# A token and channel mixer on one core: the steady part in 64-row tiles, two streams on different PSUM banks

## Chip, core and metric

The kernel runs on one core of one Trainium2 chip. The metric is the device time of one execution in microseconds; lower is better. Three runs of the kernel before gave 2051.5, 2051.76 and 2052.26 us, so the median is 2051.76 us.

## What is computed

Input `x` is 8 batches of 4096 tokens of 192 channels. First a causal local mix over 7 taps with softmaxed weights per head, then a token mix and a channel mix with ReLU, each added to what it was given. Cut to what matters:

```python
w = exp(weight_gen - max); w = w / (sum(w) + 1e-9)      # 8 heads, 7 taps
a = einsum('bshk,bskhg->bshg', w, x_unf)                # x_unf: 7 rows back from each token
h = maximum(a.transpose(0, 2, 1) @ w_tok1, 0) @ w_tok2  # 4096 -> 256 -> 4096
u = a + h.transpose(0, 2, 1)
out = u + maximum(u @ w_ch1, 0) @ w_ch2                 # 192 -> 1536 -> 192
```

The four weight matrices are float64; the kernel reads them as pairs of 32-bit words and makes float32 of them on the chip ("convert").

## The kernel before, in words

The work is cut into 64 chunks `g` of 512 tokens (8 to a batch). Every number that enters a matmul is split into a high and a low float32r part, and a product is the sum of high by high, low by high and high by low. One step on TensorE is 512 columns of one such product.

A chunk has these TensorE stages. **First channel product** (`channel1`, L735): the 1536 hidden units are 6 groups `p` of two 128-blocks; the 192 channels are three 64-row blocks. For each `p` there are 9 pairs of 64-row matmuls, one half of the array for each 128-block, each half writing its own bank of the tile `ph` (two banks). Since both halves need all 192 channels, `u` is held with its blocks copied to both halves (`u_parts`, L692: eight casts on ScalarE, two subtractions on VectorE). **Token product 2** (`token2`, L628): 10 matmuls of 128 rows into `up`, for the next chunk; ScalarE writes a seed into the tile first. **Sums** (`channel2`, L768): 10 matmuls of 128 rows for each `p`, into two accumulator banks `acc`. **Token product 1** (`token1`, L588): 16 matmuls of 128 rows and 384 or 192 columns into `th`, for a chunk of the next batch; there is one such piece a chunk until the last batch. For batch 1 (`b < F1`) it is done in plain float32 (`token1_float`, L620); the columns of a bank that a piece doesn't use are written once by extra matmuls (L608).

Between first product and sums stands `take_h` (L761): ScalarE writes the ReLU as the high part, VectorE the low part, into one of `HB` = 4 tiles `h`. `ph`, `up` and `th` share a ring of three two-bank PSUM tiles; with the two `acc` banks all eight are taken. At the end of a chunk VectorE transposes `acc` (`store`, L829) and ScalarE seeds it with the next `u` (`seed`, L822).

Order: the loop from L1324 writes each chunk's order by hand: all six first products, then token product 2 where it is ready, then the sums, with a token-1 piece where its data are ready (`picks`, L1308). In chunk 0 the first two groups are done together (`first_channel1`, L747). All engines run in program order. A planner that runs in Python while the program is built (`at`, `on`, `pump`, L868 to L978) keeps an estimate of each engine's time and fits the rest (softmax and taps for the next batch, conversions, stores) into the gaps of ScalarE and VectorE; VectorE may be filled up to `SLACK` (1500 ns) past a ReLU.

Chunk 0 runs while weights are still being converted. What is left to convert is hung on the groups `p` in a table: after `take_h` of group `p`, `run_first(p)` (L1244) puts these steps on ScalarE ("a"), VectorE ("v") and GpSimd:

```python
c21, w21, c22 = ("c2", 1), ("w2", 1), ("c2", 2)
first = {0: ((w1[2], ""),), 1: ((c2, "aa"), (c2, "v")), 2: ((c2, ""), (c21, "a")),
         3: ((c21, "aa"), (c21, "v"), (w21, "aaa"), (c21, ""), (w21, "v")),
         4: ((w21, ""), (c22, "aa")), 5: ((c22, "a"), (c22, "vw")), NP: ((c22, ""),)}
```

`w1` is the first channel matrix in three thirds, `c2` to `c22` the thirds of the second (groups 0 and 1, 2 and 3, 4 and 5), `w21` the token-2 weights of chunk 1; "" means all that is left.

Of the kernel before, what the change touches and what calls it, by code (L numbers as in the profile page):

```python
# [18 lines left out]
AX = mybir.AxisListType  # L19


@with_exitstack
def mixer_kernel(ctx: ExitStack, tc: tile.TileContext, x, wg, wt1, wt2, wc1, wc2, out):
# [14 lines left out]
    HB = 4  # L38
# [28 lines left out]
    TURN = (0, 1, 2), (1, 0, 2)  # L67
# [472 lines left out]
    def fetch_channel(which, n, tag=None):  # L540
        raw = raw_tile(tag)
        queue = nc.sync
        if which == "w1":
            dst = raw[:, 0:HF, :].rearrange("p (k n) l -> p k (n l)", k=3)
            src = wc1.rearrange("(k c) (j q n) -> j c k q n", k=3, q=NP // NC1, j=2)
            for j in range(2):
                queue.dma_start(dst[j * DC:(j + 1) * DC], src[j, :, :, n])
        else:
            c2_dma(queue, raw[:, 0:NF2 * D, :], n)
        rawt[which, n] = raw  # L550
        tag_of[which, n] = raw_tag.get(staged["raw"] - 1)
# [35 lines left out]

    def token1(m):  # L588
# [8 lines left out]
        yield  # L597
        if b >= F1:
            xh = xht.pop(m)
            for r in range(KR):  # L600
                for c in range(CT):
                    rs = slice(r * P, (r + 1) * P)
                    nc.tensor.matmul(th[:, r, 0:2 * D], w[:, c, 0, rs], xh[:, c, :], start=i + c == 0, stop=False,  # L603
                                     skip_group_check=True)
                    nc.tensor.matmul(th[:, r, 0:D], w[:, c, 1, rs], xh[:, c, 0:D], start=False, stop=c == CT - 1,  # L605
                                     skip_group_check=True)
                if m == F1 * NCH:
                    nc.tensor.matmul(th[:, r, 2 * D:], w[:, CT - 1, 0, rs], xh[:, 0, 0:N - 2 * D],  # L608
                                     start=False, stop=True, skip_group_check=True)
        else:  # L610
            token1_float(th, w, m, 0 if i == 0 else None, CT - 1)
        yield
# [6 lines left out]

    def token1_float(th, w, m, first, last):  # L620
        for r in range(KR):
            for c in range(CT):
                nc.tensor.matmul(th[:, r, 0:D], w[:, c, r * P:(r + 1) * P], xat[m][:, c, :],  # L623
                                 start=c == first, stop=c == last, skip_group_check=True)
# [3 lines left out]
    def token2(m):  # L628
# [4 lines left out]
        yield  # L633
        steps = [(n, k, d, l) for n, of in ((0, ((A_HI, 0), (A_HI, 1), (A_LO, 0))), (1, ((C_HL, 0), (C_HL, 1))))
                 for k in range(KR) for d, l in of]
        if m == 1:
            steps.sort(key=lambda s: s[3])
        for i, (n, k, d, l) in enumerate(steps):
            nc.tensor.matmul(up[:, n, :], h1[:, k, d], w[:, l, k * N:(k + 1) * N], start=False,  # L639
                             stop=n not in [s[0] for s in steps[i + 1:]], skip_group_check=True)  # L640
        yield
# [29 lines left out]

    def first_u(up):

        hi, lo = (late.tile([P, 3, N], F32R, tag=x, name=x) for x in ("u_hi", "u_lo"))
        c, e = slice(0, DC), slice(DC, P)
        uc = uf_[0][:, 1, :]
        f, g, act, dve = lo.bitcast(F32), hi.bitcast(F32), nc.scalar.copy, nc.vector
        act(hi[:, 0], up[0])
        dve.tensor_sub(lo[:, 0], up[0], hi[:, 0].bitcast(F32))
        act(hi[c, 1], g[e, 0])  # L680
        act(hi[e, 1], g[c, 0])
        dve.tensor_copy(uc[c], up[1][e])
        act(lo[c, 1], f[e, 0])
        dve.tensor_add(uc[c], up[1][c], uc[c])
        dve.tensor_copy(lo[e, 1], f[c, 0])
        act(hi[c, 2], uc[c])
        dve.tensor_copy(hi[e, 2], uc[c])
        dve.tensor_sub(lo[c, 2], uc[c], hi[c, 2].bitcast(F32))
        dve.tensor_copy(lo[e, 2], f[c, 2])
        ut[0] = hi, lo  # L690

    def u_parts(m):  # L692
# [3 lines left out]
        hi, lo = (late.tile([P, 3, N], F32R, tag=x, name=x) for x in ("u_hi", "u_lo"))  # L696
        f, act, dve = lo.bitcast(F32), nc.scalar.copy, nc.vector.tensor_sub
        left = [0, 1]
        taken = {}

        def begin():
            yield "gate", 0, lambda: state["channel1"] >= m
            yield "w", 0, lambda: free["parts"]

        def last():
            left.pop()
            if not left:
                ut[m] = hi, lo
                free["u"] = at["act"] + HOP

        def first():
            yield from begin()
            yield "u", 620, lambda: act(hi[:, 0], ua)
            yield "u", 620, lambda: act(hi[c, 2], uc[c])
            yield "n", 0, lambda: taken.update(at=at["act"] + HOP)
            yield "v", 610, lambda: dve(lo[:, 0], ua, hi[:, 0].bitcast(F32))
            yield "v", 610, lambda: dve(lo[c, 2], uc[c], hi[c, 2].bitcast(F32))
            yield "u", 620, lambda: act(lo[c, 1], f[e, 0])
            yield "u", 620, lambda: act(lo[e, 1], f[c, 0])
            yield "u", 620, lambda: act(lo[e, 2], f[c, 2])  # L720
            yield "n", 0, last

        def second():
            yield from begin()
            yield "gate", 0, lambda: "at" in taken
            yield "u", 620, lambda: act(hi[c, 1], ua[e])
            yield "u", 620, lambda: act(hi[e, 1], ua[c])
            yield "u", 620, lambda: act(hi[e, 2], uc[c])
            yield "n", 0, last
        return first(), second()  # L730


    ht, acc_t = {}, {}

    def channel1(g, p):  # L735

        u_hi, u_lo = ut[g]
        ph = ps_w.tile([P, 2, 512], F32, tag="w", name="ph")
        steps = [(w, u, k) for w, u in ((w1_hi, u_hi), (w1_lo, u_hi), (w1_hi, u_lo)) for k in range(3)]
        for n, (w, u, k) in enumerate(steps):  # L740
            for j in range(2):
                rows = slice(j * DC, (j + 1) * DC)
                nc.tensor.matmul(ph[:, j, :], w[rows, TURN[j][k], p * P:(p + 1) * P], u[rows, k], start=n == 0,  # L743
                                 stop=n == len(steps) - 1)
        return ph

    def first_channel1(ps):  # L747

        u_hi, u_lo = ut[0]
        ph = {p: ps_w.tile([P, 2, 512], F32, tag="w", name="ph") for p in ps}  # L750
        for k in range(3):
            for steps in (((w1_hi, u_hi), (w1_lo, u_hi)), ((w1_hi, u_lo),)):
                for p in ps:
                    for w, u in steps:
                        for j in range(2):
                            rows = slice(j * DC, (j + 1) * DC)
                            nc.tensor.matmul(ph[p][:, j, :], w[rows, TURN[j][k], p * P:(p + 1) * P], u[rows, k],
                                             start=k == 0 and w is w1_hi and u is u_hi, stop=k == 2 and u is u_lo)
        return ph

    def take_h(g, p, ph):  # L761
        h = ht[g, p] = big.tile([P, 2, 2, N], F32R, tag=f"h{(g * NP + p + 2) % HB}", name="h")
        nc.scalar.activation(h[:, :, 0, :], ph, AF.Relu)  # L763
# [683 lines left out]
```

## Time and profile before

| what | value |
|---|---|
| median of three runs | 2051.76 us |
| span of the profiled execution | 2049.8 us |
| TensorE matmuls busy | 2036.6 us, 99% |
| VectorE, ScalarE busy | 73%, 70% |
| GpSimd busy | 10% |
| mean granted TensorE clock | 1.000 |

The profile is of one execution. A line of a view names engine (PE is TensorE's matmuls, PEld its weight loads, DVE VectorE, ACT ScalarE, POOL GpSimd, SP the DMA queue of SyncE), source line, operation, what is written and read, and how often. Starts are microseconds from the start of the span. Ends of matmuls are modelled, so times between starts are the safe ones. A wait is given in brackets with what ended it; "issue" means that the profile shows nothing that the engine waited for.

### The profile page before, as it was taken

How to read it: one execution, taken by the hardware profiler on the slowest of the kernel's cores; microseconds unless marked ns; L12 is line 12 of the kernel's file. 1: busy time of each engine (PE TensorE's matmuls, PEld its weight loads, DVE VectorE, ACT ScalarE, POOL GpSimd, SP SyncE). 2: the span in 40 equal slices, each digit the busy share in tenths (PEclk: the TensorE clock that was granted, in tenths of full speed). 3: DMA queues.
4: the chain of work that ended last, by engine and by line, in shares of the span. 5: the costliest groups of instructions: out<-in, count | busy, mean ns of one | idle time of the engine just before them, and what ended most of it. 6: DMA issues, size and time to landing. Idle time of an engine off the chain costs nothing.

```text
span 2049.8 us, 32333 instructions
## 1 busy us (share of the span) xinstructions
PE 2036.6 (99%) x12893; PEld 1682.0 (82%) x12893; DVE 1502.7 (73%) x1740; ACT 1439.2 (70%) x2286; POOL 195.6 (10%) x260
## 2 busy tenths in 40 slices
PE   8999999999999999999999999999999999999999
PEld 8888888888888888888888888888888888888887
DVE  9979989999877787776877777877777774434343
ACT  6888767677667677677676676676676676676665
POOL 1201111111110110100110101110001110000000
PEclk9999999999999999999999999999999999999999
DMA  9948787887876666666666666766666753222121
GB/s 342 353 159 220 194 231 226 214 247 220 226 211 182 182 186 177 186 177 180 185 180 176 187 171 176 200 175 169 172 188 179 198 145 98 90 72 65 45 65 24
DMA packets 172662, 362.32 MB, mean 177 GB/s; under 512 B 28639, under 2 KB 113887, under 8 KB 156766
## 3 DMA queue, kind: packets, MB, share of 16 engines
q1 hardware_dynamic: 137342, 225.91, 35.6%
q0 software_dynamic: 34880, 134.10, 26.7%
q8 instruction: 101, 1.65, 0.3%
q14 instruction: 51, 0.42, 0.1%
q10 hardware_dynamic: 288, 0.23, 0.0%
HBM read 223.60 MB, written 71.30 MB: 144 GB/s over the span
## 4 chain that ended last, share of the span: by engine, by line
PE 94%; DVE 4%; DMA 1%; ACT 0%; issue 0%; POOL 0%; ACTq 0%; DVEq 0%
PE acc L775 41%; PE ph L743 38%; PE up L639 7%; PE th L603 4%; PE th L605 2%; DVE prk L408 1%; PE th L623 1%; PE tapsum L414 1%; DMA space<-in_x_dram 1%; PE th L1111 0%; PE acc L792 0%; DVE h L764 0%; DVE pr L266 0%; DVE vals L191 0%; DMA wg<-in_weight_gen_dram 0%
## 5 line engine op out<-in xcount | busy, mean ns | idle before, releaser
L775 PE MATMUL acc<-h,w2s 128*128 128x512 f32 x3800 | 884.7, 390 | 0.1
L775 PEld LDWEIGHTS acc<-h,w2s 128*128 128x128 f32 x3800 | 709.2, 188 | 146.5 <-issue 0.7
L763 ACT ACTIVATE h<-ph 128x1024 fp32r<-128x1024 f32 x384 | 394.3, 1027 | 345.9 <-PE ph L743 306.0
L764 DVE SCALAR_TENSOR_TENSOR h<-ph,h 128x1024 fp32r<-128x1024 f32 x384 | 468.2, 1220 | 175.7 <-ACT h L763 175.2
L743 PE MATMUL ph<-u_hi,w_hi 64*128 64x512 f32 x2292 | 330.7, 393 | 0.9 <-DVE h L764 0.9
L743 PE MATMUL ph<-u_lo,w_hi 64*128 64x512 f32 x2292 | 323.2, 387 | 0.0
L743 PE MATMUL ph<-u_hi,w_lo 64*128 64x512 f32 x2292 | 322.9, 387 | 0.0
L266 DVE TENSOR_TENSOR pr<-space,wg 128x768 f32<-128x768 f32 x336 | 311.0, 947 | 0.6
L288 POOL DMA_DIRECT2D xa<-pr x166 | 141.5, 854 | 1350.6 <-DVE pr L280 608.2
L743 PEld LDWEIGHTS ph<-u_hi,w_hi 64*128 64x128 f32 x2292 | 209.9, 184 | 65.1 <-issue 20.9
L743 PEld LDWEIGHTS ph<-u_hi,w_lo 64*128 64x128 f32 x2292 | 215.0, 184 | 46.3
L743 PEld LDWEIGHTS ph<-u_lo,w_hi 64*128 64x128 f32 x2292 | 215.2, 184 | 45.5
L846 ACT COPY out_tile<-oa 32x256 f32<-32x256 f32 x504 | 203.5, 404 | 8.1
L646 DVE TENSOR_TENSOR uf<-up,uf 64x512 f32<-64x512 f32 x63 | 43.0, 683 | 201.9 <-ACT uf L645 201.9
L639 PE MATMUL up<-w,h 128*128 128x512 f32 x630 | 161.4, 402 | 0.0
L280 DVE TENSOR_TENSOR pr<-pr 128x768 f32<-128x768 f32 x168 | 159.1, 947 | 2.3
L639 PEld LDWEIGHTS up<-w,h 128*128 128x128 f32 x630 | 114.0, 188 | 41.4 <-issue 18.3
L603 PE MATMUL th<-xh,w 128*128 128x384 f32 x384 | 112.4, 358 | 0.0
L846 ACT COPY out_tile<-oc 32x256 f32<-32x256 f32 x252 | 101.7, 403 | 4.9 <-DVE oc L839 0.4
L836 DVE STREAM_TRANSPOSE oa<-acc 128x512 f32<-128x512 f32 x63 | 45.0, 715 | 81.8 <-PE acc L775 81.8
L656 ACT COPY up<-xb 128x1024 f32<-128x1024 f32 x56 | 57.0, 1018 | 63.3 <-DVE h L764 63.3
L605 PE MATMUL th<-xh,w 128*128 128x192 f32 x384 | 96.2, 250 | 0.0
(130 smaller groups left out, 1721.9 us busy)
## 6 DMA issues: line engine op xcount, KB each, us to landing
w<-s SPq DMA_DIRECT2D x96, 1024.0 KB, 5.9
xa<-pr POOLq DMA_DIRECT2D x166, 384.0 KB, 4.8
space<-in_x_dram POOLq DMA_DIRECT2D x54, 960.0 KB, 7.9
out_dram<-out_tile SPq DMA_DIRECT2D x128, 192.0 KB, 4.0
xb<-xs SPq DMA_DIRECT2D x368, 64.0 KB, 5.0
xs<-t SPq DMA_DIRECT2D x56, 384.0 KB, 4.7
raw<-in_moe_w_tok_dram SPq DMA_DIRECT2D x16, 1024.0 KB, 8.1
s<-w POOLq DMA_DIRECT2D x8, 1024.0 KB, 8.6
```

The lines of the kernel that those rows point to most:

```text
L266: nc.vector.tensor_mul(t.rearrange("p t (h g) -> p (t h) g", h=H).rearrange("p (o n) g -> p o n g", o=1), x_k, w)
L280: nc.vector.tensor_add(sums[m], sums[m], prt.pop(m))
L288: nc.gpsimd.dma_start(xat[m].rearrange("p t d -> p (t d)"), sums[m].rearrange("p t d -> p (t d)"), accum_op=ALU.add)
L603: nc.tensor.matmul(th[:, r, 0:2 * D], w[:, c, 0, rs], xh[:, c, :], start=i + c == 0, stop=False, skip_group_check=True)
L605: nc.tensor.matmul(th[:, r, 0:D], w[:, c, 1, rs], xh[:, c, 0:D], start=False, stop=c == CT - 1, skip_group_check=True)
L639: nc.tensor.matmul(up[:, n, :], h1[:, k, d], w[:, l, k * N:(k + 1) * N], start=False, stop=n not in [s[0] for s in steps[i + 1:]], skip_gr ...
L656: nc.scalar.copy(up.rearrange("p k (n b c) -> p (k n) c b", c=CT, b=Q), xb.rearrange("p k (n c b) -> p (k n) c b", c=CT, b=Q))
L743: nc.tensor.matmul(ph[:, j, :], w[rows, TURN[j][k], p * P:(p + 1) * P], u[rows, k], start=n == 0, stop=n == len(steps) - 1)
L763: nc.scalar.activation(h[:, :, 0, :], ph, AF.Relu)
L764: nc.vector.scalar_tensor_tensor(h[:, :, 1, :], ph, 0.0, h[:, :, 0, :].bitcast(F32), op0=ALU.max, op1=ALU.subtract)
L775: nc.tensor.matmul(acc[n], w2s[:, f, d], h[:, j, l, :], start=False, stop=f == NF - 1 and i == len(steps) - 1, skip_group_check=True)
L846: nc.scalar.copy(dst, src[to:to + Q].rearrange("p (n e d) -> p n e d", n=2, d=Q)[:, n])
```

## The change

The whole steady part is done in 64-row tiles. Two streams run side by side, one on rows 0 to 63 and one on rows 64 to 127, and at any step they write different PSUM banks. A 128-row matmul becomes two 64-row ones, one in each stream, at different times.

- `emit` writes two lists of steps pairwise. Where a bank passes from one half to the other it demands more than `GAP` = 3 steps between, and puts a no-operation on TensorE's queue that waits for the old half's last matmul, unless an earlier one covers it.
- A first product has three parts (`h_steps`): each half's own 64 channels into its own bank, the last 64 channels (held in both halves), and the same own channels for the other bank. So the first two blocks of `u` need no copy in the other half; `u_parts` has four casts on ScalarE in place of eight. The rows of the first channel weights are laid out to fit (`fetch_channel`).
- A unit of the steady part is one first product beside the sums of an older group: 19 steps. One unit has token product 2 in place of the first product (20 steps). The units of a chunk are products 3, (token 2), 4, 5, and 0 and 1 of the next chunk, beside sums 0 to 5. Product 2 comes between chunks, with a token-1 piece around it or, without one, together with product 3 and sums 0 (28 steps).
- A token-1 piece is cut into two halves that stand before and after a unit.
- `HB` is 3; `u` of odd chunks takes the place of the fourth `h` tile.
- In chunk 0, products 0 to 2 come first (27 steps), then units (3, 0), (4, 1), (token 2, 2), (5, 3) and the next chunk's.

The table `first` and `run_first` are as before. The diff, cut to its core:

```diff
-    HB = 4
+    HB = 3
...
             for j in range(2):
-                queue.dma_start(dst[j * DC:(j + 1) * DC], src[j, :, :, n])
+                rows = dst[j * DC:(j + 1) * DC]
+                queue.dma_start(rows[:, 0:2], src[j, :, j:3:2 - j, n])
+                queue.dma_start(rows[:, 2], src[1 - j, :, j, n])
...
+    SIDES = [slice(j * DC, (j + 1) * DC) for j in range(2)]
+    used = {}
+    GAP = 3
+
+    def emit(*sides):
+
+        assert len(sides[0]) == len(sides[1])
+        for steps in zip(*sides):
+            used["n"] = used.get("n", 0) + 1
+            for j, (bank, out_, w, x_, start) in enumerate(steps):
+                side, n, before_ = used.get(bank, (j, 0, None))
+                if side != j:
+                    assert used["n"] - n > GAP
+                    if n > used.get("past", 0):
+                        tc.add_manual_dep(nc.tensor.nop().ins, before_.name, SYNC, reason="bank")
+                        used["past"] = n - 1
+                ins = nc.tensor.matmul(out_, w, x_, start=start, stop=False, skip_group_check=True).ins
+                used[bank] = j, used["n"], ins
...
+        def steps(n, of, j):
+            rows = SIDES[j]
+            return [(("up", m, n), up[:, n, :], h1[rows, k, d], w[rows, l, k * N:(k + 1) * N], False)
+                    for d, l in of for k in range(KR)]
...
+        yield "u", 620, lambda: act(hi[:, 0], ua)
+        yield "u", 620, lambda: act(hi[c, 1], uc[c])
+        yield "u", 620, lambda: act(hi[e, 1], uc[c])
+        yield "v", 610, lambda: dve(lo[:, 0], ua, hi[:, 0].bitcast(F32))
+        yield "v", 610, lambda: dve(lo[c, 1], uc[c], hi[c, 1].bitcast(F32))
+        yield "u", 620, lambda: act(lo[e, 1], lo[c, 1].bitcast(F32))
...
-    def channel1(g, p):
+    def h_steps(g, p, ahead):
...
+        def steps(j, at_, block, bank, start):
+            rows = SIDES[j]
+            return [(("ph", g, p, bank), ph[:, bank, :], w[rows, at_, p * P:(p + 1) * P], u[rows, block], start and i == 0)
+                    for i, (w, u) in enumerate(((w1_hi, u_hi), (w1_lo, u_hi), (w1_hi, u_lo)))]
+        own = [steps(j, 0, 0, j, j == 0 or not ahead) for j in range(2)]
+        third = [steps(j, 1, 1, j, False) for j in range(2)]
+        other = [steps(j, 2, 0, 1 - j, ahead and j == 0) for j in range(2)]
+        return ph, own, third, other
...
-    def channel2(g, p):
+    def sum_steps(g, p):
...
     for g in range(NG):
...
+        units = [(3, 0), (None, 1), (4, 2), (5, 3), (NP, 4), (NP + 1, 5)]
+        if g == 0:
+            units[1:3] = [(4, 1), (None, 2)]
+            hs = [first_product(0, p) for p in range(3)]
+            own, third, other = zip(*[h["parts"] for h in hs])
+            order = [own[0], own[1], other[0], other[1], own[2], third[0], other[2], third[1], third[2]]
+            emit(*[list(chain(*[part[j] for part in order])) for j in range(2)])
...
+            if tok is not None:
+                emit(*[h["own"][j] + tok["steps"](j, SIDES[j], True) + h["other"][j] + tok["steps"](1 - j, SIDES[j], False)
+                       for j in range(2)])
...
+                emit(both[0] + h["other"][0] + sums[0][1] + more["other"][0] + sums[0][0],
+                     both[1] + sums[1][0] + h["other"][1] + more["other"][1] + sums[1][1])
...
+            if hp is None:
+                ends.append(up_next["t"])
+                us = up_next["sides"]
+                sides = [us[0][0] + us[0][1] + sums[0][1] + sums[0][0], sums[1][1] + sums[1][0] + us[1][0] + us[1][1]]
...
+                turned = sums[1][1] + sums[1][0] + h["other"][1] + h["own"][1]
+                sides = [h["own"][0] + h["other"][0] + sums[0][1] + sums[0][0], turned]
+            if tok is not None:
+                ends.append(tok["t"])
+                sides = [tok["steps"](j, SIDES[j], True) + sides[j] + tok["steps"](1 - j, SIDES[j], False) for j in range(2)]
+            emit(*sides)
...
+                take(h, done_at, turn)
+                pump(at["dve"] + 1000, soon, free["acc"] + HOP)
+                seed(g + 1)
```

## Rows read from the trace of the kernel before

**Rows 1.** The page: engines' busy time (share of span), and granted clock in slices.
```profile
PE 2036.6 (99%) x12893; PEld 1682.0 (82%) x12893; DVE 1502.7 (73%) x1740; ACT 1439.2 (70%) x2286; POOL 195.6 (10%) x260
...
PEclk9999999999999999999999999999999999999999
```

**Rows 2.** The chain that ended last, in order of time: start, length, what.
```profile
999.35 6.80 PE acc L775 x30
...
1008.40 6.83 PE acc L775 x30
1015.23 12.49 PE ph L743 x108
1027.72 2.51 PE up L639 x10
...
1846.70 12.49 PE ph L743 x108
...
1875.30 12.49 PE ph L743 x108
```

**Rows 3.** Timeline of one `ph` stage: start, length, engine, what, xcount.
```profile
1015.16 0.97 PE L743 MATMUL ph<-u_hi,w_hi 64*128 64x512 f32 x6
...
1015.97 0.85 PE L743 MATMUL ph<-u_hi,w_lo 64*128 64x512 f32 x6
...
1018.04 0.84 PE L743 MATMUL ph<-u_hi,w_lo 64*128 64x512 f32 x6
...
1018.72 0.84 PE L743 MATMUL ph<-u_lo,w_hi 64*128 64x512 f32 x6
...
1019.60 1.03 ACT L763 ACTIVATE h<-ph 128x1024 fp32r<-128x1024 f32 x1 [0.17 <-PE ph L743]
```

**Rows 4.** Waits of the weight loads: total us, times, longest.
```profile
PEld ph L743 <- issue: 20.9, 60, 0.4
```

**Rows 5.** One line's instructions: duration ns min/median/max, first and last start.
```profile
L639 PEld LDWEIGHTS up<-w,h x630: 186/188/189, 103.3 to 2004.1; 128*128 128x128 f32 x158
...
L639 PEldq EVENT_SEMAPHORE  x57: 51/51/3631, 99.4 to 1999.6; - x57
```

**Rows 6.** Timeline of VectorE in chunk 0: weights, low parts.
```profile
87.10 0.96 DVE L211 TENSOR_TENSOR w_lo<-val,w_hi 128x768 fp32r<-128x768 f32 x1
...
92.84 1.22 DVE L764 SCALAR_TENSOR_TENSOR h<-ph,h 128x1024 fp32r<-128x1024 f32 x1
93.97 0.41 DVE L566 TENSOR_TENSOR w2s<-val,w2s 128x256 fp32r<-128x256 f32 x1
...
105.14 0.95 DVE L191 SCALAR_TENSOR_TENSOR val<-val,few 128x768 uint32<-128x768 uint32 x1
...
107.83 0.41 DVE L566 TENSOR_TENSOR w2s<-val,w2s 128x256 fp32r<-128x256 f32 x1
```

**Rows 7.** Busy time in one stretch: engines in order PE, PEld, DVE, ACT, POOL.
```profile
170.00:204.00 34.00, 34.00 (x212) 28.30 (x210) 32.20 (x40) 28.34 (x42) 5.09 (x7) 1.00 0.94 269
```

**Rows 8.** Timeline at a chunk's end and start: transpose of `acc`, its two seeds.
```profile
1015.27 0.72 DVE L836 STREAM_TRANSPOSE oa<-acc 128x512 f32<-128x512 f32 x1 [0.64 <-PE acc L775]
...
1022.69 1.11 ACT L827 COPY acc<-uf 128x512 f32<-128x512 f32 x2
```

**Rows 9.** Timeline of TensorE: the first product of chunk 0 and of chunk 1.
```profile
83.15 0.50 PE L757 MATMUL ph<-u_hi,w_hi 64*128 64x512 f32 x2
...
113.08 0.97 PE L743 MATMUL ph<-u_hi,w_hi 64*128 64x512 f32 x6
```

**Rows 10.** Timeline of ScalarE in chunk 0: conversions and the seed of `up`.
```profile
93.80 1.10 ACT L194 ACTIVATE few<-raw 128x768 f16<-128x768 f32 x1
...
95.52 1.15 ACT L192 ACTIVATE few<-raw 128x1024 uint32<-128x1024 uint32 x1
...
97.95 1.13 ACT L195 ACTIVATE val<-raw 128x1024 f32<-128x1024 f32 x1
...
101.96 1.05 ACT L654 COPY up<-xb 128x1024 f32<-128x1024 f32 x1
```

## What the change should do, predicted before it was run

> **What bounds the kernel now.** I read the page first: the shares of the engines, the slices of the granted clock. TensorE is busy for 99% of the span and at its full clock in every slice [rows 1]; no other engine passes 75%. That alone says little, since the ends of matmuls are modelled, so the next view is the chain of work that ended last, in order of time, for a chunk in the middle and one near the end [rows 2]. A chunk there is nothing but TensorE's own stages: 54 pairs of 64-row matmuls (`ph`), 10 of 128 rows (`up`), 60 of 128 rows (`acc`), and a token-1 piece. What the reader should take from it is the time of one step, 512 columns. 30 `acc` matmuls take 6.80 us, so 226.7 ns each; a pair in the middle of a `ph` stage takes the same, (1018.72 - 1018.04)/3 = 227 ns [rows 3]. Two concurrent 64-row matmuls therefore cost what one 128-row matmul costs: the rate is no argument for or against the change.
>
> The loss is at the borders. 54 pairs at 226.7 ns are 12.24 us, and the stage takes 12.49; ten steps are 2.27, and `up` takes 2.51 [rows 2]. These are the two stages that begin right after a change between 128-row and 64-row tiles, and each loses 0.25 us: the weight load sits idle for some 0.35 us with no releaser but "issue" [rows 4], and the first three pairs take 1015.97 - 1015.16 = 0.81 us in place of 0.68 [rows 3]. Two changes a chunk: 0.49 us of a late chunk's 1875.30 - 1846.70 = 28.60 us (124 steps are 28.11) [rows 2]. So nearly all of a steady chunk is steps, and what is not is the change of tile height.
>
> **The change, part by part.**
>
> *Removed: the changes of tile height.* Every step of chunks 1 to 63 becomes a pair of 64-row matmuls. 63 x 0.49 = -30.9 us. The number of steps stays: 54 + 60 + 10 a chunk and the token-1 piece.
>
> *Rate of the new pairs.* No row shows a first product beside a sum; the nearest is the pair in `ph`, which also writes two banks, at 227 ns [rows 3]. I take 227, at no cost. The bounds I set at 224 (a step that short would need part of the 13 ns beyond 512 columns at 2.4 GHz to overlap) and, on the other side, the pairs just after a change, of which the fourth to the twelfth take 1018.04 - 1015.97 = 2.07 us, 230 ns a step [rows 3].
>
> *Added: waits between the streams.* When a bank passes from one half to the other, `emit` puts a no-operation on TensorE's queue that waits for the old half's last matmul, and everything behind it on that queue waits too. Following `emit` through the order gives 33 of them in a chunk with token-1 piece and 31 without, some 2060 in all. A wait is free if it ends before the queue runs dry. The last pair of a product is the third of the group that starts at 1018.72, so it starts at 1018.72 + 2 x 0.227 = 1019.17, and ScalarE, which waits for it, starts at 1019.60: 0.43 us [rows 3]. A wait event on TensorE's sequencer takes 0.05 us [rows 5]. Banks change sides after four steps or more, and the weights for the fourth step are due three steps after the old matmul's start, at 0.68 us: 0.2 us to spare. That the sequencer's waiting need not stop the array is seen once: an event begun at 99.4 waited 3.63 us while `up`'s first load came at 103.3 behind `acc` work without a hole [rows 5]. I take 0; the bounds are 0 and 0.13 us each (weights not loaded ahead, as in the first three pairs of [rows 3]).
>
> *First products later beside older sums.* A product now ends every 19 steps (4.3 us), and its sums begin a whole unit later. ReLU 1.03 us [rows 3] and the low part 1.22 [rows 6] with two hand-overs are 2.4: 1.9 us to spare, cost 0. VectorE is the one to watch, busy 32.2 of 34 us in the stretch where batch 1 is prepared [rows 7], but the planner never lets other work run past 1.5 us after the ReLU. Token product 2 for chunk 8 now stands second in chunk 7 rather than at its end, so the last token-1 piece of batch 1 must come earlier: 0 to 6 us, I take 1.5.
>
> *Turn of the accumulator.* Two transposes (0.72) and two seeds (1.11 together) [rows 8] stood under a whole `ph` stage. Now they have 18 steps with a token-1 piece between, or 12 without. 0.43 + 1.44 + 1.11 with hand-overs is 3.1 against 12 steps and the last matmul's own, 2.95: some 0.15 us in a chunk without token-1 piece. +1.
>
> *Chunk 0.* This is where the change pays. Before, all six products (12.2 us) cover the conversion of weights that ScalarE, GpSimd and VectorE do meanwhile; from 83.15 to 113.08 the chunk takes 29.93 us for 124 steps, 1.8 over [rows 9]. The list of conversions hung on each product (`first`) is unchanged, but only three products now stand ahead of the first sums. Step by step: 27 steps end near 89.4; step 14 needs the low third of the weights that VectorE wrote at 87.10 for 0.96 us [rows 6], so 0 to 1 us late, I take 1: TensorE is free at 90.3. The sums need the first third of the second weights, written at 93.97 behind the third product's low part [rows 6], an order that stays: wait until 95.1, 4.8 us. Unit (3,0) ends at 99.4, (4,1) at 103.7. Behind the fourth ReLU ScalarE now has two conversion steps (95.52 - 93.80 = 1.72), three of the token weights (97.95 + 1.13 - 95.52 = 3.56), the fifth ReLU, two more (1.72) and the seed of `up` (1.05) [rows 10]: from 99.6, 1.03 + 1.72 + 3.56 + 1.03 + 1.72 + 1.05 = 10.1, to 109.7. Token product 2 waits 6.0. It and unit (5,3) end at 118.6; the sums of product 4 need the last third: ReLU 1.03, low part 1.22, then shift to first subtraction as at 105.14 to 108.24 (3.1 us) [rows 6], 5.4 us. Together 1 + 4.8 + 6.0 + 5.4 = 17.2, less 1.8: +15.4. Bounds: 12 (VectorE idle when its chains are due, first wait absent) and 20 (other work ahead of each).
>
> *Small ends.* A token-1 piece in two halves has two ends where the next stage runs 0.03 us over (6.83 for 6.80) [rows 2]: +2 for 56 pieces. Extra columns at the first piece of a batch: 7 times some 0.15: +1. The tail takes three products, waits for the last low part and changes tile height once: +0.8. Four casts of `u` fewer a chunk free ScalarE, which bounds nothing: 0.
>
> **Sum.** 2049.8 - 30.9 + 15.4 + 1.5 + 1 + 2 + 1 + 0.8 = 2040.6 us of span. The median of the runs shown is 2.0 above this span (2051.76), so 2042.5.
>
> *A rule that speaks against it.* The trace shows full clock throughout [rows 1], and no pause of the length of the three in chunk 0, so whether the clock falls in them no row tells. The Trainium skill, "TensorE: Matmul & The Clock Gate", section "HAM oscillation — how this bites in real kernels", says that TensorE idling for a DMA wait comes back at half clock. By the sum above chunk 0 costs 15.4; by that rule it costs more, as the third rival.
>
> **The rivals.**
> 1. *The waits bite (slower).* If a matmul's completion reaches TensorE's own queue later than the 0.68 us of three steps, the step behind each four-step hand-over starts with its weights unloaded. Seven in a chunk with token-1 piece, four without, some 420, at 0.13 us: +55, 2097 us; all 2060 would be +270. For: the sequencer, which ran some 4 us ahead [rows 5], now never can. Against: 0.2 us to spare.
> 2. *The pair gets shorter.* With streams of different operands part of the gap overlaps: 224 ns, 2.7 x 124 x 63 = -21, 2021 us. Against: the `ph` pairs do not do it.
> 3. *The pauses of chunk 0 cost double.* If the clock is at its lower level (1.2 GHz) for as much as a unit after each pause, 19 steps at 427 ns (512 columns at that level) in place of 227 add 3.8 us, three times 11.4: 2054, no change. Longer chains in chunk 0 end there too.
> That the change doesn't do what it says (128-row steps left in the steady part) is only possible at a batch's border, where a late token-1 piece runs whole: 0.5 us for the two changes, under 4 in all.
>
> **How the numbers follow.** Forecast 0.52 (2034 to 2051), rival 1 0.15, rival 2 0.20, rival 3 0.13. The range runs from rival 2 with chunk 0 at its lower bound (2017) to rival 3 with chunk 0 at its upper and some waits felt (2062); it leaves out most of rival 1. A measurement of this kernel tells 0.2%, 4 us: faster means under 2047.7, slower over 2055.9. Faster: 0.42 of the forecast, 0.20, 0.03 of rival 3: 0.65. Same: 0.10, 0.07 and 0.02 of rival 1: 0.19. Slower: 0.16.
>
> **What would show it.** In a late chunk the chain should read 28.1 us for 124 steps with no "issue" before weight loads; 28.6 would mean the loss at the borders was not the tile height. Steps over 227 ns right behind a hand-over are rival 1; steps of 224 throughout rival 2. In chunk 0 three TensorE waits of about 5, 6 and 5 us, released by VectorE's second weights, by the seed of `up`, and by the second weights again; a granted clock under 1 after them is rival 3. The forecast is wrong if VectorE or ScalarE releases TensorE in the middle of the run.

## The result, and the profile after the change

The changed kernel took 2069.51 us (median of 4 runs, 2069.11 to 2071.2), the kernel before 2052.01 us beside it: a ratio of 1.0087, 95% interval 1.0073 to 1.0102. It is slower by 0.9%, where 2042.5 us and 0.65 for faster had been predicted. The profiled execution has a span of 2068.0 us against 2049.8.

The page of the kernel after: span, busy time of TensorE, its weight loads and VectorE, and the granted clock in slices (to be read against [rows 1]).

```profile
span 2068.0 us, 43001 instructions
PE 2024.4 (98%) x18241; PEld 1730.8 (84%) x18241; DVE 1490.3 (72%) x1737; ACT 1299.6 (63%) x2033; POOL 195.2 (9%) x260
PEclk9989999999999999999999999999999999999999
```

One slice of the clock, the third, is no longer full, and TensorE's busy share fell by a point. Where, the chain and the waits tell. First the part that went as planned: from the chain of work that ended last (start, length, what), the same long piece of two late chunks, one after the other:

```profile
1872.08 2.95 PE ph L606 x26
...
1900.19 2.95 PE ph L606 x26
```

A late chunk is 28.11 us where it was 28.60 [rows 2]: 124 steps, each 226 or 227 ns after the one before, and nothing else. The waits of TensorE in the kernel after (for what; us in total, times, longest):

```profile
PE ph L606 <- DVE h L749: 9.7, 23, 0.5
PE acc L606 <- DVE w2s L568: 8.4, 2, 4.4
PE up L606 <- ACT up L669: 8.3, 1, 8.3
PE up L606 <- issue: 5.7, 1, 5.7
```

Rows two and four are chunk 0. Row two is the second weights, twice. For row four the profile names no releaser: the seed of `up` ends at 111.51 us, the low part of the token weights on VectorE at 111.48, and the first `up` matmul starts at 111.61. Row three is a pause of 8.6 us in chunk 1, row one a wait of up to half a microsecond that returns 23 times, nearly all in the steady part. The windows view shows what stands behind the pauses (stretch in us from the start: length, busy PE, PEld, DVE, ACT, POOL with counts, granted clock, DMA share, GB/s):

```profile
96.00:99.40 3.40, 3.40 (x20) 3.09 (x18) 0.00 (x0) 0.00 (x0) 0.00 (x0) 0.50 1.02 394
...
109.70:116.50 6.80, 4.89 (x23) 4.92 (x25) 2.87 (x4) 1.81 (x2) 1.05 (x2) 0.50 0.90 326
...
126.70:133.60 6.90, 5.92 (x28) 4.64 (x30) 3.60 (x6) 1.38 (x2) 0.46 (x1) 0.51 0.00 0
...
150.60:157.40 6.80, 3.46 (x16) 2.80 (x18) 2.53 (x3) 6.17 (x6) 0.00 (x0) 0.50 0.24 58
```

These are four stretches at a granted clock of 0.5, the lower level (1.2 GHz), one for each pause: the first begins 0.6 us after its pause has ended, the others within theirs. Steps there start 426 ns apart in place of 227. Counting the slow steps, they cost 1.6 + 2.2 + 2.7 + 1.6 = 8.1 us. Of the kernel before no slice shows less than full clock [rows 1].

The pause in chunk 1 is seen on ScalarE (timeline of the kernel after: start, length, engine, line, what, xcount, idle time before it and its releaser):

```profile
144.41 1.05 ACT L210 CAST w<-val 128x1024 fp32r<-128x1024 f32 x1 [2.50 <-DVE val L191]
145.49 0.81 ACT L832 COPY out_tile<-oc 32x256 f32<-32x256 f32 x2
146.31 1.65 ACT L832 COPY out_tile<-oa 32x256 f32<-32x256 f32 x4
147.98 0.82 ACT L832 COPY out_tile<-oc 32x256 f32<-32x256 f32 x2
148.81 1.65 ACT L832 COPY out_tile<-oa 32x256 f32<-32x256 f32 x4
150.48 1.12 ACT L192 ACTIVATE few<-raw 128x1024 uint32<-128x1024 uint32 x1
151.63 1.34 ACT L194 ACTIVATE few<-raw 128x1024 f16<-128x1024 f32 x1
152.85 1.04 ACT L669 COPY up<-xb 128x1024 f32<-128x1024 f32 x1
```

TensorE starts nothing between 145.30 and 153.95 us, for want of the seed of `up` (L669, the last line). What it needed besides, the weights of chunk 2, was cast at 144.41 and done on VectorE at 146.72. Between the cast and the seed stand twelve copies for the store and two steps of the next conversion, which this product does not need.

And the wait that returns, on VectorE at the end of a chunk in the middle, where the accumulator passes to the next chunk (timeline of the kernel after):

```profile
1014.75 0.96 DVE L280 TENSOR_TENSOR pr<-pr 128x768 f32<-128x768 f32 x1
1015.63 0.95 DVE L266 TENSOR_TENSOR pr<-space,wg 128x768 f32<-128x768 f32 x1
1016.50 0.71 DVE L822 STREAM_TRANSPOSE oa<-acc 128x512 f32<-128x512 f32 x1
1017.13 0.67 DVE L823 STREAM_TRANSPOSE oc<-acc 128x512 f32<-128x512 f32 x1
1017.73 1.19 DVE L749 SCALAR_TENSOR_TENSOR h<-ph,h 128x1024 fp32r<-128x1024 f32 x1
```

The last sum of the chunk starts on TensorE at 1014.05, so `acc` is ready at about 1014.5; its transposes (L822, L823) start at 1016.50, behind two pieces of attention for a later chunk. The low part of `h` (L749) stands behind the transposes, and it is this low part that frees the PSUM slot of the next first product, which starts at 1018.97. The chunks are measured here from the first `up` matmul for a chunk to that for the next; `up` for a chunk stands in the chunk before it. From `up` of chunk 11 to that of chunk 52 every second one, 21 in all, is up to 31.19 us long (every eighth 30.9, as the one shown), the ones between 30.41 (30.51 the first of a batch): 14.5 us in all. A chunk with a token-1 piece was 30.89 before.

### The profile page after: what moved, and what is told of

Read it like the earlier page. It is cut to its first block, busy times and chain, and to the rows that moved or that the text cites. A ratio compares the mean times of both kernels' runs of the same rounds, so it can differ in the third digit from the quotient of the medians.

```text
span 2068.0 us, 43001 instructions
## 1 busy us (share of the span) xinstructions
PE 2024.4 (98%) x18241; PEld 1730.8 (84%) x18241; DVE 1490.3 (72%) x1737; ACT 1299.6 (63%) x2033; POOL 195.2 (9%) x260
## 4 chain that ended last, share of the span: by engine, by line
PE 70%; DVE 24%; ACT 3%; issue 2%; DMA 1%; POOL 0%; ACTq 0%; DVEq 0%
PE acc L606 32%; PE ph L606 26%; PE up L606 7%; DVE pr L266 7%; DVE h L749 5%; PE th L606 4%; DVE pr L280 4%; DVE xa L266 2%; DVE prk L408 1%; DVE xh L340 1%; PE tapsum L414 1%; DVE oa L822 1%; DVE u L721 1%; DVE oc L823 1%; ACT uf L660 1%
## 5 line engine op out<-in xcount | busy, mean ns | idle before, releaser
L606 PE MATMUL acc<-h,w2s 64*128 64x512 f32 x7620 | 1666.2, 388 | 8.4 <-DVE w2s L568 8.4
L606 PEld LDWEIGHTS acc<-h,w2s 64*128 64x128 f32 x7620 | 1333.9, 185 | 144.8 <-DVE w2s L568 4.9
L606 PE MATMUL ph<-u,w_hi 64*128 64x512 f32 x4608 | 1367.4, 389 | 9.7 <-DVE h L749 9.7
L606 PEld LDWEIGHTS ph<-u,w_hi 64*128 64x128 f32 x4608 | 774.4, 184 | 94.5 <-DVE h L749 15.2
L606 PE MATMUL ph<-u,w_lo 64*128 64x512 f32 x2304 | 812.3, 387 | 0.3 <-DVE w_lo L211 0.3
L749 DVE SCALAR_TENSOR_TENSOR h<-ph,h 128x1024 fp32r<-128x1024 f32 x384 | 465.3, 1212 | 286.3 <-ACT h L745 285.4
L606 PEld LDWEIGHTS ph<-u,w_lo 64*128 64x128 f32 x2304 | 389.7, 185 | 38.1 <-DVE w_lo L211 0.8
L606 PE MATMUL up<-w,h 64*128 64x512 f32 x1260 | 300.7, 390 | 13.9 <-ACT up L669 8.3
L606 PEld LDWEIGHTS up<-w,h 64*128 64x128 f32 x1260 | 234.6, 186 | 37.1 <-ACT up L669 8.7
L606 PEld LDWEIGHTS th<-xh,w 64*128 64x128 f32 x1548 | 119.5, 185 | 7.9
L606 PE MATMUL th<-xh,w 64*128 64x384 f32 (+2 forms) x1548 | 123.6, 298 | 0.0
L822 DVE STREAM_TRANSPOSE oa<-acc 128x512 f32<-128x512 f32 x63 | 44.8, 711 | 59.9 <-PE ph L606 59.7
```

The lines of the kernel that those rows point to most:

```text
L606: ins = nc.tensor.matmul(out_, w, x_, start=start, stop=False, skip_group_check=True).ins
L749: nc.vector.scalar_tensor_tensor(h[:, :, 1, :], ph, 0.0, h[:, :, 0, :].bitcast(F32), op0=ALU.max, op1=ALU.subtract)
L822: nc.vector.transpose(ua, acc[0])
```

## Experiments

Each edit is made to the changed kernel, and beside each stand runs of the kernel before (medians 2052.05 to 2052.53 us). step_128, step_64 and nops3 have one execution each.

### The first term: what a change of tile height costs

`zero` is a block of zeros. The first added line is step_128, the other two are step_64:

```diff
  emit(*sides)
+ nc.tensor.matmul(acc_t[g][0], zero, ut[g][0][:, 0], start=False, stop=False, skip_group_check=True)  # step_128
+ emit(*[[(("acc", j), acc_t[g][j], zero[SIDES[j]], ut[g][0][SIDES[j], 0], False)]       # step_64
+        for j in range(2)])
```

> One addition to the changed kernel: behind each of 370 units stands one product of a block of zeros by u into acc, 128 rows high and 512 columns long; it adds nothing to the sums. So TensorE goes from 64-row tiles to a 128-row tile and back 370 times more. Theory (each passage costs 0.25 us, the first term of the prediction's sum: 0.49 a chunk for two): 370 x (0.227 + 0.49) = 265 us more, about 2335 us, and a late chunk grows by 0.72 us for each of its units. Rival (a passage costs nothing by itself; what the late chunks gained came from another edit): 84 us more, 2153 us, 0.23 us for each unit.

> The control for the one before it: at the same 370 places a pair of products of zeros by u, each 64 rows high, one on each bank of acc, so one step more and no passage to 128 rows. Both theories: 370 x 0.227 = 84 us more, 2153 us, less up to 5 us where the alternating stall takes it in; a late chunk grows by 0.23 us for each of its units. If a step of 64-row pairs cost more at such places than inside a unit, this would be higher, and the difference to the one before is what a passage costs.

Measured: 2296.3 us with the 128-row steps, 2138.45 with the 64-row pairs. From the chains, two late chunks of each (first step_128, then step_64):

```profile
2140.77 3.17 PE ph L606 x25
...
2172.18 3.17 PE ph L606 x25
```

```profile
1904.53 2.72 PE ph L606 x24
...
1933.77 2.72 PE ph L606 x24
```

31.41 and 29.24 us for five places in a chunk. Against 28.11, a pair more costs (29.24 - 28.11)/5 = 0.226 us, a plain step; a 128-row step costs (31.41 - 28.11)/5 = 0.66, so the two passages cost 0.43 us. Over the run it is (2296.3 - 2138.45)/370 = 0.427, the same. How the 0.43 us divide, a timeline of TensorE in step_128 shows (L1393 is the 128-row step; of the two lines of each pair one is copied):

```profile
2125.06 0.39 PE L606 MATMUL ph<-u,w_hi 64*128 64x512 f32 x1
2125.37 0.50 PE L1393 MATMUL acc<-u,zero 128*128 128x512 f32 x1
2125.80 0.50 PE L606 MATMUL ph<-u,w_hi 64*128 64x512 f32 x1
...
2126.14 0.39 PE L606 MATMUL ph<-u,w_lo 64*128 64x512 f32 x1
2126.37 0.39 PE L606 MATMUL ph<-u,w_hi 64*128 64x512 f32 x1
```

From the last pair to the 128-row step 0.31 us, from there to the next pair 0.43, and 0.34 to the one after: 1.08 for three steps of 0.227, so 0.40 of the 0.43. It was 0.49 a chunk in the kernel before, where whole stages met. The price of a change of tile height is a cost of its own, and the first term stands. The forecast of 2335 us was too high by 39: 23.5 since two passages cost 0.427 and not 0.49 (370 x 0.063), and 14.5 since the wait that returns in the changed kernel is gone here. step_64 too came out 14.6 under its 2153, where at most 5 had been allowed for that wait. With a step more in each unit the chunks in the steady part are 31.77 us (31.87 the first of a batch), which is 30.41 + 6 x 0.227, with no long one between. Of the 9.7 us that TensorE waited for the low part of `h` this is left in step_64:

```profile
PE ph L606 <- DVE h L749: 0.3, 1, 0.3
```

### Rival 1: the waits between the streams

```diff
- tc.add_manual_dep(nc.tensor.nop().ins, before_.name, SYNC, reason="bank")
+ for _ in range(3):
+     tc.add_manual_dep(nc.tensor.nop().ins, before_.name, SYNC, reason="bank")
```

> One edit to the changed kernel: each wait of TensorE for its own earlier product (some 32 a chunk, put where a bank passes from one stream to the other) is issued three times. Theory (such a wait costs nothing where the product lies four steps or more back): a late chunk, without token product 1, stays at 28.107 us = 124 steps of 226.67 ns, the time at 2069.5 us. Rival (rival 1 of the prediction, each costs what an event semaphore took on TensorE in the trace of before, 51 ns): 64 more x 51 ns = 3.3 us a chunk, over 2200 us; and the changed kernel would then owe 1.6 us a chunk to the waits it has.

Measured: 2069.71 us, but the run does not test what it was made for. Its page, and the waits that stand by themselves at the changed line, in the changed kernel (L604) and in nops3 (L605; number, duration in ns, first and last start):

```profile
span 2067.9 us, 43001 instructions
```

```profile
L604 PEldq EVENT_SEMAPHORE  x198: 51/51/51, 87.2 to 2050.1; - x198
...
L605 PEldq EVENT_SEMAPHORE  x198: 51/51/51, 87.2 to 2050.0; - x198
```

There are 43001 instructions, as many as in the changed kernel. By the semaphores that TensorE's instructions name, both traces also have the same 2020 waits for TensorE's own matmuls, 1819 of them on weight loads. So the trace has no sign of the added waits.

What speaks against rival 1 is the changed kernel itself. Its late chunk from 1900.19 us has 30 such waits, and all its 124 steps start 226 or 227 ns apart, behind a hand-over as elsewhere. So the waits that it has cost nothing there, and rival 1 falls; what more of them would cost stays open.

### The clock behind the pauses

```diff
+ for _ in range({(0, 0): 16, (0, 2): 24, (0, 4): 18, (1, 1): 35}.get((g, cp), 0)):
+     nc.tensor.matmul(acc_t[g][0], zero, ut[g][0][:, 0], start=False, stop=False, skip_group_check=True)
  emit(*sides)
```

> One addition to the changed kernel: ahead of the four units of chunks 0 and 1 at which TensorE stands still (4.4, 6.1, 4.8 and 8.6 us), 16, 24, 18 and 35 products of a block of zeros by u are added to acc, 227 ns each, so 3.6, 5.4, 4.1 and 7.9 us of each pause are filled with work that adds nothing. Theory (the clock falls because TensorE stood still): none of the four stretches at a granted clock of 0.5 (96.0 to 99.4, 109.7 to 116.5, 126.7 to 133.6, 150.6 to 157.4 us) is left, their 426 ns steps become 227 ns, and the 1.6 + 2.2 + 2.7 + 1.6 = 8.1 us come back: about 2061 us, with the waits of the pauses ending when they did. Rival (the clock falls with the conversions and transfers of these chunks, whatever TensorE does): the stretches stay, and products of zeros at half clock outlast the pauses: 2070 us or more.

`zero` is a block of zeros as above. Measured: 2061.06 us (ratio to before 1.0042, 1.0027 to 1.0057), 8.45 less than the changed kernel. The same windows, of this kernel:

```profile
96.00:99.40 3.40, 3.40 (x34) 3.27 (x32) 0.00 (x0) 0.00 (x0) 0.00 (x0) 1.00 0.95 384
...
109.70:116.50 6.80, 6.75 (x59) 6.78 (x61) 1.56 (x3) 1.69 (x3) 0.53 (x1) 1.00 0.84 270
...
126.70:133.60 6.90, 6.90 (x64) 6.32 (x62) 4.43 (x6) 3.08 (x3) 0.05 (x1) 1.00 0.30 100
...
150.60:157.40 6.80, 6.80 (x64) 5.62 (x62) 5.58 (x8) 5.08 (x7) 0.00 (x0) 1.00 0.75 214
```

TensorE has its full clock in all four, and no conversion or transfer of these chunks was left out; 8.1 us had been worked out from the slow steps. So it is TensorE's standing still that costs the clock. The Trainium skill, "TensorE: Matmul & The Clock Gate", section "HAM oscillation — how this bites in real kernels", says this of a wait for a DMA; the trace agrees, here for waits on ScalarE and VectorE.

### The pause in chunk 1

```diff
- def pump(limit, keys=(), scalar_limit=float("inf")):
+ def pump(limit, keys=(), scalar_limit=float("inf"), until=None):
...
-     while True:
+     while until is None or not until():
...
-         pump(at["pe"] + SLACK, keys)
+         pump(at["pe"] + SLACK, keys, until=what)
```

> One edit to the changed kernel: where the planner must have something (here the second-layer weights of the next chunk, converted, ahead of a token product 2), it stops handing work to ScalarE and VectorE as soon as it has it. In the changed kernel it went on there, in chunk 1, and 12 store copies and two steps of the next conversion (145.49 to 152.85 us on ScalarE) stood ahead of the seed of up, so TensorE stood still from 145.30 to 153.95 us. Theory (the order on ScalarE makes the pause, not the conversion): the seed comes at about 145.5, the last conversion step ends at 146.7 on VectorE, the pause shrinks from 8.6 to about 1.5 us, and the stretch at half clock behind it (150.6 to 157.4 us, worth some 1.6 us) goes too: 2069.5 - 7.1 - 1.6 = about 2061 us. Rival (the conversion itself is late, or the displaced store copies make the next token product late): the pause stays above 6 us or returns in chunk 2, 2067 to 2070 us.

Measured: 2068.45 us (ratio 1.0081, 1.0066 to 1.0096): only 1.1 us less. The time is the rival's, but not for the rival's reason. The pause in chunk 1 did go as the first theory says (ScalarE, timeline of need_stop):

```profile
144.60 1.05 ACT L210 CAST w<-val 128x1024 fp32r<-128x1024 f32 x1 [2.50 <-DVE val L191]
145.55 1.01 ACT L669 COPY up<-xb 128x1024 f32<-128x1024 f32 x1
```

The seed follows the cast, TensorE waits 0.9 us instead of 8.4, and the two chunks from `up` of chunk 1 to `up` of chunk 3 take 63.7 us in place of 72.7: 9.0 less, where 8.7 had been worked out. But the next nine chunks take 293.8 in place of 285.3, nearly all of it at one place (VectorE, timeline of need_stop):

```profile
391.23 0.96 DVE L280 TENSOR_TENSOR pr<-pr 128x768 f32<-128x768 f32 x1
398.15 0.96 DVE L266 TENSOR_TENSOR xa<-space,wg 128x768 f32<-128x768 f32 x1 [5.97 <-DMA space<-in_x_dram]
399.03 0.71 DVE L822 STREAM_TRANSPOSE oa<-acc 128x512 f32<-128x512 f32 x1
```

The planner had put a piece of attention ahead of the transposes of `acc`; the rows of x that it needs came 11.85 us after their load was issued (386.29 to 398.14), and the planner counts 9 us, 12 at the border of a batch. VectorE stood still for 5.97 us; TensorE started nothing for 6.2 us and then ran its steps at half clock for 5 us. To see whether the load was the cause, the count was raised:

```diff
  (the edit of need_stop, and)
- LOAD_X, LOAD_B = 9000, 12000
+ LOAD_X, LOAD_B = 13000, 14000
```

> The edit of need_stop (the planner stops when it has what it must have) and, beside it, the planner counts 13 and 14 us for a load of x instead of 9 and 12. Theory (the 6.2 us pause that need_stop had at 395 us came from one load of x, 11.85 us long, for which VectorE stood still with the transposes of acc behind it, since the planner counted 9 to 12 us): that pause and its stretch at half clock go, 8 us, and chunk 1's 9 us stay gained: 2060 us. Rival (the order of chunks 7 and 8 is too full on VectorE, whatever the load): a pause of some us stays there, 2065 us or more.

Measured: 2066.17 us (1.0067, 1.0049 to 1.0085), on the rival's side of the line. The pause of 6.2 us is gone, so the load did make it; but the nine chunks still take 291.0 us, with gaps of 1.2, 1.6 and 1.4 us on TensorE in two of them. VectorE was nearly full in such a stretch of the kernel before too, 32.2 of 34 us [rows 7]; that work taken out of one place came back in another here is argued from that, not shown.

### The wait that returns

```diff
  elif not last and (not following or more == 5):
-     pump(done_at + TOP + SLACK, soon, done_at - 900)
+     pump(done_at + TOP + SLACK if following else end, soon, done_at - 900)
```

> One edit to the changed kernel: at the last unit of a chunk the planner fills VectorE with background work up to the unit's end, no longer up to 2.5 us past it, so that the two transposes of acc and the low part of h behind them are not late. Theory (VectorE's order at the turn makes the alternating stall): the chunks of 31.153 us fall to the 30.414 us of their neighbours, 21 x 0.74 = about 15 us less, 2055 us, with VectorE's low part no longer among the releasers of the first product's ring slot (now 23 waits). Rival (the stall is a matter of load, and the displaced work comes late in another place, or the first product waits for something else next): under 5 us gained, 2065 us or more.

Measured: 2057.07 us (10 runs, 2054.45 to 2059.93; ratio 1.0022, 1.0012 to 1.0032), 12.4 less. From `up` of chunk 12 to that of chunk 56 the chunks are 30.41 us (30.51 the first of a batch, 31.03 one), 1339.3 us in place of 1352.5: the theory holds, 13.2 us came back there. In the traced execution (2059.84 us, among the longest of the ten) some of it was given up ahead of that, at another late load of x in chunk 9 (chain of turn_end):

```profile
414.82 11.32 DMA space<-in_x_dram
...
426.16 0.96 DVE xa L266
427.12 1.15 DVE h L749
```

### Chunk 0, and all orders together

```diff
  first_u(up)
+ act(c2, 2)
  rest(w1[1])
  dve(w1[2])
+ dve(c2)
...
- first = {0: ((w1[2], ""),), 1: ((c2, "aa"), (c2, "v")), 2: ((c2, ""), (c21, "a")),
-          3: ((c21, "aa"), (c21, "v"), (w21, "aaa"), (c21, ""), (w21, "v")),
-          4: ((w21, ""), (c22, "aa")), 5: ((c22, "a"), (c22, "vw")), NP: ((c22, ""),)}
+ first = {0: ((c2, ""),), 1: ((w1[2], ""),),
+          2: ((c21, "aaa"), (c21, "v"), (w21, "aaa"), (c21, ""), (w21, "v")),
+          3: ((w21, ""), (c22, "aaa"), (c22, "v")), 4: ((c22, ""),)}
```

> One edit to the changed kernel, in the order of chunk 0's conversions alone: the steps for the first third of w2s stand ahead of the first ReLU, those for its second third and for token product 2's weights in the 7.2 us in which ScalarE otherwise waited for the ReLU of unit (3, 0), those for its last third behind that ReLU. Nothing is left out. Theory (chunk 0's pauses come from the order on ScalarE and VectorE, which idled 7.2 and 7.4 us each twice while conversions stood behind a ReLU): the pauses of 4.4, 6.1 and 4.8 us shrink to about 1, 1.5 and 0, so -12.8, and the three stretches at half clock behind them (6.5 us) go: about 2050 us. Rival (the conversions' own throughput sets the pauses, whatever their order): the three pauses move, and together stay above 10 us: 2062 to 2070 us.

Measured: 2054.19 us (10 runs, 2050.25 to 2055.47; ratio 1.0008, 0.9999 to 1.0018), 15.3 less, where 19 had been expected, so most of the pauses came from the order. The terms differ from those expected: steps of TensorE start 0.8, 3.2 and 2.9 us apart where the pauses of 4.4, 6.1 and 4.8 stood (1, 1.5 and 0 were expected), with half clock behind the last two. The pause in chunk 1 went as well: the weights of chunk 2 were done on VectorE at 127.84 us in place of 146.72. Gaps of 1.2, 2.9 and 1.2 us at 129.6, 159.1 and 195.7 us stand in the chunks that follow instead. What is left in chunk 0, from the waits of TensorE in early:

```profile
PE up L606 <- ACT up L669: 2.8, 1, 2.8
PE ph L606 <- DVE u L721: 2.5, 1, 2.5
```

The second is `u` of chunk 1: it is made from token product 2, and only one unit, (5, 3), stands between that and its first use.

Then the three orders together (early, need_stop, turn_end), once with the longer count for a load of x and once without:

> Three orders mended at once in the changed kernel: chunk 0's conversions early, the planner's stop when it has what it must have (chunk 1), VectorE filled only to the end of a chunk's last unit; and the planner counts 13 and 14 us for a load of x instead of 9 and 12, since one took 11.85 us where VectorE stood still for it in the second of these edits alone. No product, copy or transfer is added or left out. Theory (the change is worth its 30.9 us of switches, and what it lost lay in orders around it): 2069.5 - 19 (chunk 0, with its clock) - 9 (chunk 1, with its clock) - 14 (alternating stall) = about 2027 us, under the kernel before by 25 us. Rival (each mended order makes another thing late, as the pause of 6 us in chunk 8 that came with the second edit): 2040 us or more.

> The kernel of all_three with the planner's count for a load of x left at 9 and 12 us. If the longer count carried part of its gain, a pause returns (2 to 8 us: 2034 to 2040 us); if the three orders carry it alone, 2032 us as there.

Measured: 2032.28 us with it (ratio 0.9903, 0.9889 to 0.9918; 2027 had been expected), 2044.81 without (0.9964, 0.9950 to 0.9977). The first beats both kernels, by 1.0% and 1.8%. The count for the load carries 12.5 us of it, far more than I had given it: without it a gap of 2.6 us stands in chunk 7, and in chunk 15 the last token-1 piece of the next batch is so late that token product 2 starts 4.4 us after the step before it, with steps at half clock behind both. The span of all_three is 2029.6 us; from its waits:

```profile
PE up L606 <- POOL w2s L215: 2.9, 1, 2.9
PE ph L606 <- DVE u L721: 2.5, 1, 2.5
```

These are the longest two, both in chunk 0; every chunk from the eleventh on is 30.41 us (30.51 or 30.55 the first of a batch), or 28.11. The span is 11 us under the 2040.6 that the sum gave, of which 9.8 are chunk 0's pauses: 0.5, 0.6, 0.6, 3.0 and 2.7 us, 7.4 together, for the 17.2 of the sum. One stretch at half clock is left in it, behind the last of these.

## Why the prediction was wrong

By the steps of its sum:

- **Changes of tile height, -30.9: right.** Late chunks 28.60 to 28.11, chunks with a token-1 piece 30.89 to 30.41; the passage measured by itself costs 0.43 us for two.
- **Rate of the new pairs, 227 ns: right**, so rival 2 falls. **Waits between the streams, 0: right**, so rival 1 falls. The working took each to be an instruction of its own on TensorE's queue; 1819 of the 2020 sit on weight loads.
- **Chunk 0, +15.4: right in place, cause and nearly in size.** The pauses predicted were 1, 4.8, 6.0 and 5.4 us; TensorE's gaps over a step are 0.51 and 0.53 at the start, then 4.20, 5.84 and 4.59: 15.7 for 17.2. Those of 4.20 and 4.59 were released by the second weights, as named; at that of 5.84 the seed of `up` came last by 0.03 us, and the profile names no releaser.
- **The clock behind these pauses: put at nothing in the sum**, given as rival 3 with 0.13. It was set aside because no row of before has such a pause. Rival 3 worked out 11.4 us for three; it is 6.5 for those three, since the stretches were 8 to 14 slow steps long and not 19, and 8.1 with the one in chunk 1.
- **Chunk 1: put at nothing, without a reason.** I saw that token product 2 now stands second in its chunk, and followed it for chunk 7 only (the +1.5). In chunk 1 its weights are still being converted, so the planner is made to wait for them, and while it waits it hands out everything that it has. That cost 8.4 us; need_stop shows it in that chunk.
- **Turn of the accumulator, +1: the term that was furthest off.** It counted 0.43 + 1.44 + 1.11 from the end of the last sum and so took VectorE to be free then. The step above it even gives the reason, "the planner never lets other work run past 1.5 us after the ReLU": at a middle unit that margin lies behind a low part that follows the ReLU, at the turn the two transposes and the low part stand behind it. So each second turn was late by up to 0.8 us, 14.5 in all; turn_end gave 13.2 back.
- **Small ends:** the halves of token-1 pieces +1 (+2 was given: 0.49 gained in a late chunk, 0.47 in one with such a piece, 55 times), extra columns some +0.7 if all seven cost what can be read at five of them, 30.51 for 30.41 us (+1 was given).

Put together: 2040.6 - 1.5 (chunk 0) + 8.1 (clock) + 8.4 (chunk 1) + 13.5 (turn, 14.5 for 1) - 1 - 0.3 (small ends) = 2067.8, against the span of 2068.0. The border of the batch (+1.5) and the tail (+0.8) stand in this as they were forecast; they were not singled out, and that the sum comes out so close is no proof of them.

Of what would show the forecast wrong the last sentence came true: VectorE released TensorE in the middle of the run, 23 times. The chance for slower, 0.16, stood on the waits between the streams (0.13) and on the clock in chunk 0 (0.03). The places where the reordering could make an order late that was written for the old one had been priced at 1 us (the turn) and 1.5 us (chunk 7), or, in chunk 1, not at all, and none was a rival.

Why every second turn: the kernel prepares its softmax for two chunks at a time, and VectorE has more behind it in one of the two. That is argued from the order, not shown by a run.

## What to carry to other kernels

A change of order on the engine that sets the pace moves its hand-overs, and what was laid out for the old order (a list of conversions, a planner's margin, a count for a load) can then be late. Price each such order at its own place, above all what stands in another engine's queue ahead of the work that TensorE waits for. A pause of TensorE costs more than its length when the clock falls with it, so pauses are to be kept out of the start of the kernel as much as out of its middle. When an edit is meant to multiply something, count it in the trace of the edited kernel before reading its time. When one late order is mended, look at the whole trace again before judging the edit: need_stop gained 9 us in two chunks and lost 8.6 in the next nine.

## What the hardware showed that was not expected

The clock does not go by the length of a pause alone. In turn_end a single gap of 2.3 us was followed by steps at half clock (windows view, as above):

```profile
428.30:431.00 2.70, 2.69 (x14) 2.15 (x16) 2.67 (x5) 0.79 (x1) 0.85 (x1) 0.55 1.00 388
```

In all_three a gap of 3.25 us at 100.0 was not, and one of 2.9 us twelve us later was:

```profile
103.30:112.00 8.70, 8.70 (x77) 8.70 (x79) 2.98 (x6) 1.79 (x3) 0.00 (x0) 1.00 0.74 252
115.50:118.40 2.90, 2.90 (x14) 2.31 (x16) 0.52 (x1) 2.29 (x3) 0.00 (x0) 0.50 0.00 0
```

In early and in three_no_lead the gap at that same place, 3.17 and 3.19 us long, was followed by steps at half clock. What decides stays open. And products of zeros, which change no sum, are a way to hold the clock over a pause that cannot be removed: 93 of them gave back 8.45 us.
